# A linear-attention recurrence with a token and channel mixer: block triangular inverse, whole-partition evictions and a remade instruction order

## The chip, the cores and the metric

The kernel runs on one core of a Trainium2 chip. The metric is the device time of one execution in microseconds. The core's engines are TensorE (PE in the profile; PEld is its weight load), VectorE (DVE), ScalarE (ACT), GpSimd (POOL) and SyncE (SP), which issues most DMAs.

## The reference

Two parts follow one another. The first is a gated recurrence over 768 time steps for 4 batches and 8 heads with a 40 x 40 state. The second is a mixer over tokens and channels.

```python
def _attn_ref(r, k, v, w, a, b):           # each 4 x 8 x 768 x 40, float32
    state = zeros(B, H, D, D)
    for t in range(S):
        y[:, :, t] = einsum('bhd,bhde->bhe', r_t, state)
        Sa = einsum('bhde,bhe->bhd', state, a_t)
        state = state * w_t[:, :, None, :] - einsum('bhd,bhe->bhde', Sa, b_t)
        state = state + einsum('bhd,bhe->bhde', v_t, k_t)

def _moe_ref(x, w_tok1, w_tok2, w_ch1, w_ch2):   # x is y as 4 x 768 x 320
    h = relu(x.transpose(0, 2, 1) @ w_tok1) @ w_tok2       # 768 -> 256 -> 768
    u = x + h.transpose(0, 2, 1)
    h2 = relu(u @ w_ch1) @ w_ch2                            # 320 -> 1536 -> 320
    return u + h2
```

## The kernel before

**Chunks.** The 768 steps of a batch are cut into 12 chunks of 64, so there are 48 chunks in all, handled two by two as 24 pairs. Inside a chunk the recurrence is written with matrices: a 64 x 64 strictly triangular matrix per head must be inverted, and then a chunk needs a few matmuls and one state from the chunk before. Two heads stand on top of one another in the partitions: rows 0 to 39 hold one, rows 64 to 103 the other, and four such pairs of heads lie side by side.

**Preparation (t_pre, t_a).** For a pair, running products of the gates are formed by a scan (L552, L645), and the inputs are scaled by them (AB and KBp at L491, on DVE or POOL as the settings p_a and p_k say for each batch). Matmuls of L715 give the products px, whose two halves go to XT (masked, L727), NB (L733, L735) and Dg. Dg holds the diagonal 32 x 32 blocks. They stand alternately in the first and in the second 32 columns, and so four evictions of 32 partitions each bring them over (L746 on ACT or L748 on DVE).

**The solve (t_solve).** The chunks are solved in eight sets (of 4, 6, 6, 6, 6, 6, 6 and 8 chunks). DVE transposes the diagonal blocks (DT, L785) and inverts them: fifteen steps by rows, each a product (L808) and a sum (L810) over two 16 x 16 blocks at a time, of 2t^2 elements in step t. From the fourth set on, DVE also joins the 16 x 16 blocks to 32 x 32 (L823, L825, L836, L839); in the first three sets TensorE does that (merge). Two transposes give TBn and TBt (L871, L866).

**The chain (t_chain, t_s, t_rm, t_y).** For every chunk: z from XT, W, AB and the state (L1046), its eviction ZS (L1068, L1070), U and its transpose (L1082, L1085) in two PSUM banks, one for each of the two heads of a pair, U's two evictions to W (L1095, L1096), the transpose's two evictions to VT (L1166), and the new state ST (L1124, L1126, L1133). A copy of the state is spread into a block form (SS, L1152). VT and RB give RM (L1183), which is masked (L1200, or copied by ACT and masked by POOL at L1210 as rmp says), and L1237 and L1242 give y.

**The mixers (t_mlp).** One for each batch, started when its twelve chunks are done; the last one takes its tokens as they come. TensorE works with float32r operands split into a high and a low part. Settings say where an eviction goes: hdp (of a hidden tile's low part: DVE at L1640, or ACT and POOL at L1635) and c2p (of the second product: DVE at L1680, or ACT at L1674 and POOL at L1677), each with one number for each batch. The split weights are made in the kernel too (t_piece): 32 pieces are loaded by SP (L1321), converted by ACT, DVE (L1334, L1335, L1337) and POOL (L491), and stored to DRAM by SP (L1349).

**The order.** The program's order on every engine is made by a planner in the kernel's own Python. It simulates the engines with fixed prices, gives every step a rank (mostly in units of chunks) and lets each engine take the ready step of the lowest rank. The settings K hold ranks, spans, buffer counts and the choice of engines. A step that lists both ACT and DVE goes to the one that can take it. The conversion of weights has a gate:

```python
yield K_ready[min(K["conv_after"], NPR - 1)]
```

Of the kernel before, what the change touches and what calls it, by code (L numbers as in the profile page):

```python
# [24 lines left out]
LAT = {"PE": 190.0, "ACT": 210.0, "DVE": 130.0, "POOL": 150.0, "SP": 40.0, "SWD": 100.0}  # L25


K = dict(kw=4300.0, kwn=2, kw1=188.93925028732068, wug=10.0, ld0=0.6317250924768794, ldw0=2.1173303662595164,
         fgap=293.89554076183873, keep=3800.0, entry=3700.0, cold=0, hold=2428.165163486685, la=2.175877794961337,
         lw=-0.14323384525040384, le=1051.2152564940388, la_pe=-1.466665252232031, lw_pe=-37.533348810551956,  # L30
         lat=[200.0, 150.0, 145.0, 90.0], aff=1.4651042617773267, sets=[4, 6, 6, 6, 6, 6, 6, 8], nxt=8, nkp=2, nkb=12,
         rmp=[0, 0, 2, 0], hdp=[0, 1, 1, 1], c2p=[0, 0, 0, 1], npt=4, ld=6.038928624718252, ldv=4.00699059428611,
         pl=[-0.9477378132052551], ptl=3.6069776451328477, xtl=1.8544356360912841, kbl=-1.3723067761040764,
         op1=('ACT','DVE',), slack=-13908.358498323609, evm=15.481077541396273, slack_c=3496.0790885208608, p_a=[1, 2,
         1, 0], p_k=[0, 1, 1, 0], solve=[3.4390776166284533, 1.7006518949949656, 4.274466296951854, 2.435219810738553,
         3.4275080414655226, 5.510007117082695, -4.084092431783224, 0.1424821572249326], solve_span=9.61372691238832,
         atomic=1, a=8.22737306035122, a_span=3.1925291387789234, b=0.280588932000626, chain=-0.267542847460926,
         pu=-0.4315673334223724, rml=-1.6506651065553348, nw2=3, nvt=3, nrb=3, nrm=3, nss=2, evac=-4.311312911607387,
         y=-1.9244399780387127, utr=-6.460258455178398, pem=3, mrg=2.9201745296420394, ea=10, w=3, c=2, m=2, fill=300,
         alt_c=0, fill_cols=2692.2446469651372, mlp=[12.176995908837672, 28.35767213986017, 33.82155643447318,  # L40
# [1827 lines left out]
```

## Time and profile before

| | |
|---|---|
| time, median of 3 runs | 823.57 us (818.12 to 823.77) |
| the profiled execution's own time | 824.24 us |
| its span | 822.5 us |
| TensorE busy (matmuls) | 706.1 us, 86%, 14474 matmuls |
| TensorE weight loads | 633.0 us, 77% |
| DVE busy | 616.4 us, 75%, 1372 instructions |
| ACT busy | 338.9 us, 41%, 976 |
| POOL busy | 230.6 us, 28%, 252 |
| DMA | 129.22 MB, mean 157 GB/s |

The span runs from the first to the last instruction. Matmuls are pipelined, so a busy TensorE isn't one at its peak. Busy shares are means over the whole; the stages differ.

### The profile page before, as it was taken

How to read it: one execution, taken by the hardware profiler on the slowest of the kernel's cores; microseconds unless marked ns; L12 is line 12 of the kernel's file. 1: busy time of each engine (PE TensorE's matmuls, PEld its weight loads, DVE VectorE, ACT ScalarE, POOL GpSimd, SP SyncE). 2: the span in 40 equal slices, each digit the busy share in tenths (PEclk: the TensorE clock that was granted, in tenths of full speed). 3: DMA queues.
4: the chain of work that ended last, by engine and by line, in shares of the span. 5: the costliest groups of instructions: out<-in, count | busy, mean ns of one | idle time of the engine just before them, and what ended most of it. 6: DMA issues, size and time to landing. Idle time of an engine off the chain costs nothing.

```text
span 822.5 us, 33224 instructions
## 1 busy us (share of the span) xinstructions
PE 706.1 (86%) x14474; PEld 633.0 (77%) x14474; DVE 616.4 (75%) x1372; ACT 338.9 (41%) x976; POOL 230.6 (28%) x252
## 2 busy tenths in 40 slices
PE   3178757779887998999988899999999999999996
PEld 2167647668776887888877779888888888889996
DVE  6898898886778995998898789984499855445222
ACT  4237444434457334344344564544443222333221
POOL 4017655555655211012122022212101110102231
PEclk9999999999999997999997999999999999999999
DMA  9345773566679542445384464453664323445341
GB/s 248 90 145 146 225 225 110 174 190 182 199 232 299 170 160 85 153 128 162 109 269 134 138 187 146 140 172 96 195 197 128 116 79 106 140 136 164 113 147 52
DMA packets 61416, 129.22 MB, mean 157 GB/s; under 512 B 6864, under 2 KB 40912, under 8 KB 58192
## 3 DMA queue, kind: packets, MB, share of 16 engines
q1 hardware_dynamic: 54928, 79.85, 32.9%
q0 software_dynamic: 6336, 47.19, 17.6%
q8 instruction: 115, 1.88, 1.0%
q14 instruction: 37, 0.30, 0.1%
HBM read 108.33 MB, written 18.68 MB: 154 GB/s over the span
## 4 chain that ended last, share of the span: by engine, by line
PE 45%; DVE 29%; DMA 11%; issue 8%; ACT 3%; POOL 2%; SPq 1%; DVEq 0%; POOLq 0%; ACTq 0%
PE bkm L1505 8%; PE bkm L1616 7%; PE bkc L1505 4%; PE bkw L1616 4%; DMA cv_c<-in_moe_w_ch_dram 3%; PE bkw L367 3%; PE bkw L715 3%; DVE tmp L808 2%; DMA sG<-cv_c 2%; DVE Tl L810 2%; PE bkc L1082 2%; PE bkw L1183 2%; DMA sT<-cv_t 2%; PE bkc L1111 2%; DVE tmp_y L836 2%
## 5 line engine op out<-in xcount | busy, mean ns | idle before, releaser
L1616 PE MATMUL bkm<-ut,wg_c 128*128 128x384 f32 x560 | 120.3, 352 | 4.0 <-DVE hd L1640 1.4
L1505 PE MATMUL bkm<-wg_c,hd 128*128 128x320 f32 x621 | 110.3, 322 | 4.0 <-DVE hd L1640 2.6
L1616 PEld LDWEIGHTS bkm<-ut,wg_c 128*128 128x128 f32 x560 | 95.5, 189 | 9.0 <-DVE hd L1640 2.2
L1505 PEld LDWEIGHTS bkm<-wg_c,hd 128*128 128x128 f32 x621 | 92.7, 190 | 9.2 <-DVE hd L1640 4.8
L491 POOL TENSOR_TENSOR cv_c<-cv_c 128x384 f32<-128x384 f32 (+3 forms) x72 | 70.7, 998 | 53.7 <-ACT cv_c L1339 21.3
L1625 ACT ACTIVATE hd<-bkm 128x384 fp32r<-128x384 f32 x70 | 34.4, 491 | 115.8 <-PE bkm L1616 107.3
L1183 PE MATMUL bkw<-RB,VT 40*64 40x64 f32 x1536 | 51.9, 258 | 7.0 <-ACT VT L1166 4.6
L1439 POOL DMA_DIRECT2D wg_c<-sG x32 | 18.2, 569 | 138.3 <-PE bkm L1505 53.6
L1082 PE MATMUL bkc<-ZS,TBD 64*64 64x40 f32 x768 | 44.7, 257 | 11.9 <-DVE ZS L1070 6.0
L1680 DVE TENSOR_TENSOR x<-bkm,x 128x320 f32<-128x320 f32 x69 | 33.4, 485 | 26.6 <-PE bkm L1505 26.1
L1082 PEld LDWEIGHTS bkc<-ZS,TBD 64*64 64x64 f32 x768 | 37.0, 165 | 20.9 <-DVE ZS L1070 7.7
L1635 POOL TENSOR_TENSOR hd<-h,hd 128x384 fp32r<-128x384 f32 x24 | 25.2, 1049 | 89.5 <-issue 57.7
L367 PE MATMUL bkw<-ident,KBp 104*128 104x104 f32 x192 | 32.4, 329 | 20.7 <-issue 7.3
L1183 PEld LDWEIGHTS bkw<-RB,VT 40*64 40x64 f32 x1536 | 41.0, 163 | 10.9 <-ACT VT L1166 5.1
L808 DVE TENSOR_TENSOR tmp<-Tl,DT 128x2 f32<-128x2 f32 (+14 forms) x120 | 46.0, 383 | 2.2
L1242 PE MATMUL yb<-KT,RM 128*64 128x40 f32 x768 | 45.2, 244 | 0.7 <-POOL RM L1210 0.5
L491 POOL TENSOR_TENSOR AB<-AB,w 104x512 f32<-104x512 f32 x15 | 20.0, 1331 | 87.6 <-DVE w L552 85.3
L367 PEld LDWEIGHTS bkw<-ident,KBp 104*128 104x128 f32 x192 | 25.9, 186 | 23.8 <-issue 13.3
L1242 PEld LDWEIGHTS yb<-KT,RM 128*64 128x64 f32 x768 | 41.3, 163 | 1.1 <-POOL RM L1210 0.8
L810 DVE TENSOR_REDUCE Tl<-tmp 128x2 f32<-128x2 f32 (+14 forms) x120 | 38.6, 322 | 2.4
L1085 PE MATMUL bkc<-TBD,ZS 64*40 64x64 f32 x768 | 39.5, 254 | 0.7 <-issue 0.7
L715 PE MATMUL bkw<-AB,KBp 40*64 40x64 f32 x1408 | 37.2, 272 | 3.0 <-DVE XT L727 1.6
(184 smaller groups left out, 1783.8 us busy)
## 6 DMA issues: line engine op xcount, KB each, us to landing
wg_c<-sG POOLq DMA_DIRECT2D x16, 1152.0 KB, 6.4
wg_c<-sG POOLq DMA_DIRECT2D x16, 960.0 KB, 5.3
KBp<-in_kbT_dram SPq DMA_DIRECT2D x24, 448.0 KB, 4.7
wg_t<-sT POOLq DMA_DIRECT2D x8, 1152.0 KB, 6.1
W<-in_vt_dram SPq DMA_DIRECT2D x48, 160.0 KB, 3.2
w<-in_wT_dram SPq DMA_DIRECT2D x24, 224.0 KB, 2.9
wr<-in_wT_dram SPq DMA_DIRECT2D x24, 224.0 KB, 2.8
AB<-in_aT_dram SPq DMA_DIRECT2D x24, 224.0 KB, 3.7
```

The source lines that it names most:

```text
L367: nc.tensor.matmul(out_, lhsT=in_, rhs=idn, start=True, stop=True, is_transpose=True)
L491: return [(e, Port(60 + f * n / 0.96 if e == "DVE" else 140 + 2.24 * n), lambda e=e: engines[e].tensor_tensor(out=out_(), in0=a_(), in1=b_ ...
L715: nc.tensor.matmul(d["px"][i][0][o0:o0 + 64, z, p, :], lhsT=KBp[q][rows(r), p, z, i ^ r, :], rhs=AB[q][rows(r), p, z], start=True, stop=True)
L808: lambda tmp: tt(out=vw(tmp), in0=tv[:, :, 0:t, 0:t], in1=dv[:, :, t, 0:t].unsqueeze(2).to_broadcast([128, 2, t, t]), op=ALU.mult),
L810: lambda tmp: nc.vector.tensor_reduce(out=tv[:, :, 0:t, t], in_=vw(tmp), axis=AX.X, op=ALU.add),
L1082: nc.tensor.matmul(ub[r][0][bs, 0, p, 0:D], lhsT=oq["tbd"][bs, z, p, :], rhs=d["zs"][bs, p, :], start=True, stop=True)
L1085: nc.tensor.matmul(ub[r][0][rows(r), 1, p, :], lhsT=d["zs"][bs, p, :], rhs=oq["tbd"][bs, z, p, :], start=True, stop=True)
L1183: nc.tensor.matmul(bk[r][0][i * 64:i * 64 + 64, p, :], lhsT=o["vt"][rows(r), int(i != r), p * C:p * C + C], rhs=o["rb"][rows(r), p * C:p * ...
L1242: nc.tensor.matmul(py[g - 1][z * 64:z * 64 + 64, h, :], lhsT=RMs[g - 1 + z][:, h, :], rhs=st[g - 1 + z]["kb"][:, h, :], start=zero, stop=z ...
L1505: nc.tensor.matmul(d[key], lhsT=lhs(i, a_), rhs=rhs(i, b_), start=i == 0 and j == 0, stop=i == n - 1 and j == 2)
L1616: nc.tensor.matmul(pt, lhsT=mm_[q][0], rhs=mm_[q][1], start=q == 0, stop=q == len(mm_) - 1)
L1625: nc.scalar.activation(out=hid[key][:, 0], in_=pt, func=AF.Relu)
```

## The change

- **The inverse.** Row steps run only to 8 columns, on four 8 x 8 blocks at once (4t^2 elements in step t, t from 1 to 7). Then a copy of 128 elements and four steps of 512 elements (two "left", two "right", each a product and a sum) give the off-diagonal 8 x 8 blocks of the 16 x 16 ones.
- **Diagonal blocks.** One eviction of all 128 partitions brings the first 32 columns, multiplied by a factor for each partition that is -1 or 0; the other blocks are added from NB, multiplied by a factor that is 1 or 0 (e4).
- **State spread.** Both evictions read all 104 partitions and multiply by a 0/1 factor for each partition.
- **U transposed.** One PSUM bank holds U of both heads, the other holds the transposes; one eviction of all partitions goes to VT, and each bank is given back on its own.
- **Matmul rows.** The operands of several matmuls now take rows 0 to 63 and 64 to 103 or 111, where it was 40 rows of each; the rows between are zero in one of the operands.
- **The order.** Prices in the planner (DMA latencies, some instructions, TensorE's forms) and nearly all ranks are others. Settings by batch: c2p, hdp, rmp, p_k; conv_after is 1 and was 3. A form of the XT eviction that goes over ACT and POOL exists (xtp), and isn't used.

The long lists of numbers are shortened and rounded here.

```diff
-LAT = {... "SP": 40.0, "SWD": 100.0}
+LAT = {... "SP": 500.0, "SWD": 400.0}
...
-K = dict(kw=4300.0, ... keep=3800.0, entry=3700.0, ... nkb=12, rmp=[0, 0, 2, 0], hdp=[0, 1, 1, 1], c2p=[0, 0, 0, 1],
-         p_k=[0, 1, 1, 0], ... ea=10, fill_cols=2692, mlp=[12.18, 28.36, 33.82, 56.89], mlp_span=[13.5, 8.5, 12.4, 84.4],
-         conv_t=9.89, conv_t_span=-57.57, conv_c=4.67, conv_c_span=14.81, conv_after=3)
+K = dict(kw=3600.0, ... keep=3600.0, entry=3450.0, ... nkb=11, rmp=[0, 0, 2, 1], xtp=[0, 0, 0, 0], hdp=[1, 1, 1, 1], c2p=[0, 3, 3, 1],
+         p_k=[0, 0, 2, 0], ... ea=8, fill_cols=4332, mlp=[10.76, 28.78, 33.44, 51.80], mlp_span=[17.6, 7.9, 14.1, 89.7],
+         conv_t=9.96, conv_t_span=-56.49, conv_c=4.13, conv_c_span=17.91, conv_after=1)
...
+    def wrows(r, n=LP):
+        return slice(r * 64, 64 if r == 0 else n)
...
-                        nc.tensor.matmul(d["px"][i][0][o0:o0 + 64, z, p, :], lhsT=KBp[q][rows(r), p, z, i ^ r, :],
-                                         rhs=AB[q][rows(r), p, z], start=True, stop=True)
+                        nc.tensor.matmul(d["px"][i][0][o0:o0 + 64, z, p, :], lhsT=KBp[q][wrows(r), p, z, i ^ r, :],
+                                         rhs=AB[q][wrows(r), p, z], start=True, stop=True)
...
-        def e3(b, e):
-                sl, c0 = slice(b * L, b * L + L), (b & 1) * L
-                dst, src = Dgs[si % 2][sl, ci * NP:(ci + 2) * NP], kb_[sl, :, c0:c0 + L]
+        def e3(e):
+            dst, src = Dgs[si % 2][:, ci * NP:(ci + 2) * NP], kb_[:, :, 0:L]
+            if e == "ACT":
+                return ("ACT", act(256), lambda: nc.scalar.activation(out=dst, in_=src, func=AF.Copy, scale=mev[:, 0:1]), tb)
...
+        def e4():
+            dst = Dgs[si % 2][:, ci * NP:(ci + 2) * NP]
+            return ("DVE", Port(dve(256)), lambda: nc.vector.scalar_tensor_tensor(out=dst, in0=o["nb"], scalar=mod[:, 0:1], in1=dst, op0=ALU.mult, op1=ALU.add))
...
-        now = yield [[e3(b, "ACT"), e3(b, "DVE")] for b in range(4)] + [("DVE", dve(256), e2, tb) if ea else ("ACT", act(256), e2, tb)]
+        now = yield [[e3("ACT"), e3("DVE")], ("DVE", dve(256), e2, tb) if ea else ("ACT", act(256), e2, tb)]
         P.rel(tb, now)
+        now = yield [e4()]
...
-                    return tmp[:, 0:2 * t * t].rearrange("p (q j s) -> p q j s", q=2, j=t)
+                    return tmp[:, 0:4 * t * t].rearrange("p (q j s) -> p q j s", q=4, j=t)
...
+            def left8(q):
+                return step(
+                    lambda tmp: tt(out=cube(tmp), in0=dv[:, q, 8:16, 0:8].unsqueeze(2).to_broadcast(sh8),
+                                   in1=tv[:, q, 0:8, 0:8].unsqueeze(1).to_broadcast(sh8), op=ALU.mult),
+                    lambda tmp: nc.vector.tensor_reduce(out=d["Y"][:, 2 + q].rearrange("p j t -> p t j"), in_=cube(tmp), axis=AX.X, op=ALU.add),
+                    512, f"tmp{i}_l{q}", 1.1)
...
-            steps = [row(t) for t in range(1, 16)]
+            steps = [row(t) for t in range(1, 8)] + [[("DVE", Port(210), t22)]]
+            steps += [left8(0), left8(1), right8(0), right8(1)]
...
-            ub = yield from banks("c", [128, 2, NP, C], [f"u{g}", f"ut{g}"])
+            (u_, uk), (t_, tk) = yield from banks("c", [128, NP, C], [f"u{g}", f"ut{g}"])
...
-                (nc.scalar.copy if e == "ACT" else nc.vector.tensor_copy)(out=SS[g + 1][rows(r), :, r], in_=p_[rows(r)])
+                    nc.scalar.activation(out=SS[g + 1][:, :, r], in_=p_[0:DP], func=AF.Copy, scale=mhd[:, r:r + 1])
...
-        now = yield [[uc(r, "ACT"), uc(r, "DVE")] for r in range(2)]
-        yield u_ev
-        for _, k_ in ub:
-            P.rel(k_, now)
+        now = yield [[uc("ACT"), uc("DVE")]]
+        P.rel(tk, now)
```

## Rows read from the trace of the kernel before

**Rows 1.** Stretches: length, busy us (instructions) of each engine, PEclk, DMA share, GB/s

```profile
0.00:267.00 267.00, 184.11 (x5132) 165.02 (x5132) 219.88 (x488) 125.90 (x350) 132.73 (x141) 1.00 0.64 189
267.00:823.00 556.00, 521.97 (x9346) 467.97 (x9344) 396.56 (x885) 213.03 (x627) 97.85 (x112) 0.97 0.46 141
735.00:823.00 88.00, 80.75 (x548) 78.81 (x545) 26.72 (x59) 25.38 (x67) 19.82 (x25) 0.98 0.38 122
20.00:61.00 41.00, 18.82 (x500) 16.48 (x498) 37.10 (x79) 11.74 (x36) 4.44 (x4) 1.00 0.40 119
```

**Rows 2.** Waits of TensorE, 0 to 267 us: total us, times, longest us

```profile
PE bkw L919 <- DVE TBn L871: 22.6, 2, 17.5
```

**Rows 3.** Waits of TensorE, 267 to 823 us

```profile
PE bkc L1082 <- DVE ZS L1070: 4.1, 5, 1.9
```

**Rows 4.** L715, min/median/max ns in three stretches, and one stretch

```profile
L715 PE MATMUL bkw<-AB,KBp x448: 283/311/366, 63.0 to 248.3; 40*64 40x64 f32 x150
L715 PE MATMUL bkw<-AB,KBp x64: 311/311/344, 319.9 to 321.6; 40*64 40x64 f32 x64
L715 PE MATMUL bkw<-AB,KBp x320: 218/218/268, 466.2 to 560.6; 40*64 40x64 f32 x160
317.20:327.50 10.30, 10.30 (x220) 9.10 (x219) 4.94 (x10) 4.49 (x13) 0.00 (x0) 0.50 0.21 64
```

**Rows 5.** Timeline of DVE in the first solve: start us, length us

```profile
28.02 0.11 DVE L808 TENSOR_TENSOR tmp<-Tl,DT 128x2 f32<-128x2 f32 x1
...
32.59 0.37 DVE L808 TENSOR_TENSOR tmp<-Tl,DT 128x200 f32<-128x200 f32 x1
...
33.38 0.41 DVE L808 TENSOR_TENSOR tmp<-Tl,DT 128x242 f32<-128x242 f32 x1
...
37.54 0.63 DVE L808 TENSOR_TENSOR tmp<-Tl,DT 128x450 f32<-128x450 f32 x1
...
38.74 0.16 DVE L643 TENSOR_TENSOR D<-rq,PC 104x8 f32<-104x8 f32 x1
```

**Rows 6.** Groups by line and shape: busy us, mean ns, idle before

```profile
L746 ACT ACTIVATE Dg<-bkw 32x256 f32<-32x256 f32 x76 | 28.5, 375 | 18.6 <-PE bkw L715 17.9
L989 ACT COPY ET<-bkw 128x256 f32<-128x256 f32 x24 | 8.8, 367 | 7.1 <-PE bkw L983 6.7
L965 ACT ACTIVATE TBD<-TBt,blk 128x256 f32<-128x256 f32 x18 | 8.8, 506 | 9.4 <-DVE TBt L866 3.5 <-DVE TBt L939 3.1 <-DVE rq L640 1.9
L1335 DVE SCALAR_TENSOR_TENSOR cv_t<-cv_t 128x384 int32<-128x384 int32 x8 | 4.6, 573 | 0.6 <-ACT cv_t L1333 0.6
L1166 ACT COPY VT<-bkc 40x256 f32<-40x256 f32 x59 | 21.6, 366 | 1.0 <-DVE W L1096 0.2
L1166 DVE COPY VT<-bkc 40x256 f32<-40x256 f32 x37 | 15.6, 422 | 2.3 <-ACT W L1095 1.2
L1680 DVE TENSOR_TENSOR x<-bkm,x 128x320 f32<-128x320 f32 x69 | 33.4, 485 | 26.6 <-PE bkm L1505 26.1
L1677 POOL TENSOR_TENSOR x<-x,c 128x320 f32<-128x320 f32 x8 | 7.0, 871 | 32.1 <-ACT c L1674 32.1
L1635 POOL TENSOR_TENSOR hd<-h,hd 128x384 fp32r<-128x384 f32 x24 | 25.2, 1049 | 89.5 <-issue 57.7 <-ACT h L1632 31.8
L491 POOL TENSOR_TENSOR KBp<-KBp,wr 104x1024 f32<-104x1024 f32 x12 | 29.8, 2486 | 30.2 <-DVE wr L645 20.1 <-DMA KBp<-in_kbT_dram 5.0 <-PE bkc L1046 3.7
```

**Rows 7.** Groups by line: two operations of one size, over the whole span

```profile
L1126 DVE TENSOR_TENSOR ST<-bkc,ST 104x160 f32<-104x160 f32 x40 | 12.6, 316 | 9.8 <-PE bkc L1111 8.1 <-issue 1.3 <-ACT sp L1465 0.2
L1133 DVE TENSOR_TENSOR ST<-ST,PC 104x160 f32<-104x160 f32 x40 | 19.4, 486 | 0.6
```

**Rows 8.** Timeline around the gate of the conversion and the first state

```profile
16.93 1.23 DVE L491 TENSOR_TENSOR KBp<-KBp,wr 104x1024 f32<-104x1024 f32 x1 [1.56 <-DMA KBp<-in_kbT_dram]
...
54.05 2.91 SPq L1321 DMA_DIRECT2D cv_t<-in_moe_w_tok_dram  x4
...
73.61 0.33 DVE L1124 TENSOR_TENSOR ST<-bkc,PC 104x160 f32<-104x160 f32 x1 [0.88 <-PE bkc L1111]
```

More of the change, by code (lines that the diff above doesn't have):

```diff
@@ L24 @@
         "Q": (262.0, 340.0)}
[L25 to L40, printed above, removed]
-         56.88923782707786], mlp_span=[13.530525442548209, 8.457019380212113, 12.416974889480139, 84.37794635100765],
-         conv_t=9.890090295257227, conv_t_span=-57.567106844583016, conv_c=4.670000090481311,
-         conv_c_span=14.8116671529059, conv_after=3)
@@ L333, in run @@
             left[0] -= 1
-            left[1] = max(left[1], (end or t0 + ns) + (LATP[self.form][not self.warm] if e == "PE" else self.lat[eng]))
+            left[1] = max(left[1], (end or t0 + ns) + (LATP[self.form][not self.warm] if e == "PE" else self.lat[eng] + 1600.0 * (eng == "SP" and t[0].gi_code.co_name == "t_piece")))
             if left[0] == 0:
@@ L423, in tile_kernel @@
         nc.gpsimd.memset(blk0[q * 64:q * 64 + L], 1.0)
+    mev, mod = ctile([128, 1], "mev"), ctile([128, 1], "mod")
+    nc.gpsimd.tensor_scalar(out=mev, in0=blk0, scalar1=-1.0, scalar2=None, op0=ALU.mult)
+    nc.gpsimd.tensor_scalar(out=mod, in0=blk0, scalar1=-1.0, scalar2=1.0, op0=ALU.mult, op1=ALU.add)
+    mhd = ctile([DP, 2], "mhd")
+    nc.gpsimd.memset(mhd, 0.0)
+    for h in range(2):
+        nc.gpsimd.memset(mhd[h * 64:h * 64 + D, h:h + 1], 1.0)
     PC = ctile([DP, NG, NP], "PC")
@@ L573, in sq @@
                 nc.scalar.activation(out=jk, in_=d["wr"], func=AF.Square, accum_out=CE[bi][1][:, j:j + 1])
-            now = yield [("ACT", 525, sq)]
+            now = yield [("ACT", 616, sq)]
             P.set(sq_ev, now)
@@ L1143, in f @@
                 for r in range(2):
-                    nc.tensor.matmul(p_[rows(r), p, :], lhsT=ST[g + 1][rows(r), p, :], rhs=sel[rows(r), :], start=True, stop=True)
+                    nc.tensor.matmul(p_[rows(r), p, :], lhsT=ST[g + 1][wrows(r, DP), p, :], rhs=sel[wrows(r, DP), :], start=True, stop=True)
             return f
-        now = yield mm4([pu(p) for p in range(NP)], 77, 133, 94, "Q", 8)
+        now = yield mm4([pu(p) for p in range(NP)], 77, 133, 130, "Q", 8)
         P.set(PU_done[g + 1], now)
@@ L1182, in f @@
                     for i in range(2):
-                        nc.tensor.matmul(bk[r][0][i * 64:i * 64 + 64, p, :], lhsT=o["vt"][rows(r), int(i != r), p * C:p * C + C],
-                                         rhs=o["rb"][rows(r), p * C:p * C + C], start=True, stop=True)
+                        nc.tensor.matmul(bk[r][0][i * 64:i * 64 + 64, p, :], lhsT=o["vt"][wrows(r), int(i != r), p * C:p * C + C],
+                                         rhs=o["rb"][wrows(r), p * C:p * C + C], start=True, stop=True)
             return f
-        now = yield mm4([rr(p) for p in range(NP)], 142, 214, 258, "Q", 16)
+        now = yield mm4([rr(p) for p in range(NP)], 142, 214, 275, "Q", 16)
         P.rel(R_vt, now)
```

124 lines of the change are left out of this document (83 added, 41 removed).

## The prediction

> **What bounds the kernel now.** I read the stretches first: each row gives the length of the stretch, the busy time of TensorE, of its weight loads, of VectorE (DVE), ScalarE (ACT) and GpSimd (POOL), the granted clock and the DMA share [rows 1]. They show two different kernels. Up to 267 us TensorE is busy for 184.1 us and idle for 83, while DVE is busy for 219.9 us (82%), ACT for 125.9 and POOL for 132.7. From 267 us to the end TensorE is busy for 522.0 of 556 us and idle for 34. Of those 34, 7 lie in the stretch from 735 us, in which only the last mixer is left; the recurrence can move about 27.
>
> Next I read who keeps TensorE waiting. In the first stage one wait stands out: 22.6 us, in two pieces, the longer 17.5 us, for TBn, at the end of the triangular solve [rows 2]. In the second stage the longest entry is 4.1 us in five pieces [rows 3]. So a cheaper eviction can't win much by itself there, and in the first stage it wins only if it brings a solve or a chunk forward.
>
> Last I read TensorE's clock. The matmuls of L715 took 311 ns in the first stage. They took 311 ns also in a stretch where the granted clock was 0.50, and 218 ns in the stretch from 460 to 600 us [rows 4], in a stage whose mean is 0.97 [rows 1]. The 1.00 in the row of the first stage [rows 1] contradicts this; I go by the durations and take the first 267 us to run at the lower level. So work that moves out of that stage, or a stage that ends earlier, is worth its time, and a stretch at the lower level in the second stage costs 1 - 218/311 = 30% of its length.
>
> **The solve by rows to 8 and by blocks to 16.** The old rows run from 28.02 to 38.74 us in the first set: 10.7 us for fifteen steps, 2 x (1 + 4 + ... + 225) = 2480 elements in each of the two operations [rows 5]. The step of 200 elements takes from 32.59 to 33.38, 0.79 us; that of 450 from 37.54 to 38.74, 1.20 us. That is 0.00164 us an element and 0.46 us a step, and 15 x 0.46 + 2480 x 0.00164 = 11.0, close to 10.7. New: seven steps on four blocks, 4 x 140 = 560 elements, 7 x 0.46 + 0.92 = 4.1 us; four steps of 512, 4 x (0.46 + 0.84) = 5.2 us; one copy of 128 elements, which I put at 0.3. Sum 9.6, so 1.1 us a set is saved, 9 us of DVE over eight sets. In set 0 TensorE stands still for it, so 1.1 us counts in full. Sets 1 and 2 also lie in the first stage and the second piece of the TBn wait is one of theirs: 2 us of 2.2 counts. The five later sets are hidden behind a busy TensorE: 0, and at most 5.5 if that cover went.
>
> **Diagonal blocks in whole partitions.** Each of 24 pairs had four evictions of 32 partitions, 80 on ACT (76 of them in the row) at 375 ns and 16 on DVE, which I put at 0.4 us [rows 6]: 30 + 6.5 us. New are one eviction of 128 partitions and one addition from SBUF (e4). A longer partition range costs nothing on ACT: 256 elements on 32 partitions take 375 ns and on 128 partitions 367 (L989); with the factor read from a tile, as the new one has it, 506 (L965). So the eviction costs 9 to 12 us in all. The addition isn't in the trace; the nearest row is L1335, the same operation with 384 elements, 573 ns. Bounds for 256 elements are 0.28 and 0.57 us; I take 0.40, 9.6 us on DVE. ACT falls by about 19 us and DVE rises by about 3; at the lower bound it rises by nothing. A pair's path from matmul to solve shortens from five evictions in a row to three operations, some 0.7 us, which matters in set 0 alone and is inside the order's term below.
>
> **U transposed.** 96 copies become 48: 59 on ACT at 366 ns and 37 on DVE at 422 [rows 6], 37.2 us, halved: ACT -11, DVE -8. All of it in the second stage is covered. The two halves of U now share one PSUM bank, so their evictions go one behind the other; the bank is free without waiting for the low-ranked copy of the transpose. The one is worth up to +0.3 us a chunk, the other as much the other way; I take 0, with +/-4 us for the twelve chunks of the first stage. **State spread**: the same 88 evictions with a factor read from a tile; by L965 against L746 up to +0.13 us each, 11 us of ACT at most and hidden, since ACT is busy for less than half of either stage [rows 1]. **Whole row ranges in the matmuls** (64 or 48 rows for 40): the same count of instructions; L715 itself fixes no price for rows, so 0, bounds +/-3 us.
>
> **What the new settings move.** c2p for mixers 1 and 2 takes 48 additions from DVE (485 ns, L1680) to ACT and POOL (871 ns, L1677): DVE -23, POOL +42 [rows 6]. hdp for mixer 0: 8 subtractions to POOL at 1049 ns (L1635), +8, DVE -4. rmp for batch 3: 12 masks go from DVE to a copy on ACT and a product on POOL, of 256 elements and so below L1635's time: at most 1 us each, POOL +10, DVE some -5. p_k goes the other way: the six KBp products of batch 1 leave POOL (2.49 us each [rows 6]) for DVE (1.23 [rows 8]), +7 on DVE, half of it in the first stage; those of batch 2 may go to either. In the first stage alone DVE gets: rows -3.3, transposes -2.3, diagonal +1, KBp +3.7, so about -1. **The operations alone free nothing there**; the second stage loses some 30 us of DVE work, which TensorE's 27 us of idle time hardly sees.
>
> The moved POOL work can come back as waits. L1133 and L1126 are the same size; L1126 reads one input from PSUM and takes 316 ns in the mean; L1133 reads both from SBUF and takes 486, 170 ns more [rows 7]. The Trainium skill has a rule on this (SBUF — State Buffer, section Who interferes with whom): a DVE instruction with two SBUF inputs is locked out while a GpSimd instruction reads SBUF, one with a single SBUF input is not. The trace agrees, and the rule speaks against this change. Its price from rows is the second rival below.
>
> **The order.** Every instruction's place changes, and the trace of before shows no part of that; here I choose between bounds. In the first stage the conversion of weights waits until KBp of the fourth pair is done: its first four loads go out at 54.05 us. With conv_after 1 they may start when the second pair's is done, at 16.93 + 1.23 = 18.2 us [rows 8], at a time when POOL (4.4 of 41 us) and ACT (11.7) are mostly idle [rows 1]; the conversions of the channel weights are ranked later (last rank 21.5 for 19.0). SP is ahead of nothing it wasn't ahead of, but its queue then has cv_t loads beside those of w, AB and KBp. The product that makes the first state starts at 73.61 us [rows 8]. I take -5 us for the first stage, with bounds of -15 (a fifth of its idle time) and +12 (third rival below). In the second stage, -5 of the 27 us idle (bounds 0 and -12), and -3 for one stretch of 10.3 us at the lower clock [rows 4] that a denser order avoids (bounds -7 and +6, two stretches fewer or more).
>
> **Sum.** 824.24 - 1.1 - 2 - 5 - 5 - 3 = 808.1 us against the profiled execution, which lies 0.7 us above the median of the runs; forecast 808.
>
> **Rivals.** (1) Hidden: the removed work was covered, and the new order is as good as the old. Then only the solve's 3 us remain: 821. For it: TensorE is 94% busy from 267 us. Against it: 83 us of idle time before. (2) The port: some 60 us of POOL work is added in the second stage, 11% of it, to a POOL that was busy for 28% of the whole, so L1133's loss of 170 ns would grow by four tenths, 0.07 us. DVE has 885 instructions there [rows 1]; if half of them read two inputs from SBUF they lose 31 us together, which eats the relief, and if TensorE waits for a quarter of it the time is 824 - 3 + 8 = 829, within 1%. (3) **Slower: the conversions start too early.** DVE is busy for 37.1 of the 41 us from 20 to 61 us [rows 1]. Eight cv_t conversions need three DVE operations each, about 0.5 us apiece (L1335: 573 ns [rows 6]), 12 us in all. If the order puts them ahead of the preparation for the first two sets, the first state's product comes at 86 us and not 74, and everything behind it moves: 824 - 3 + 12 = 833. It decides as soon as more than some 8 of those 12 us stand before the first state. (4) The new solve does not get shorter, if strided 8 x 8 operands cost DVE more an element than rows do: nothing gained, 824.
>
> **How the numbers follow.** A measurement of this kernel tells 1% from no change. The forecast's case (better order, 790 to 815) gets 0.56; hidden 0.20 and the port 0.05 and no shorter solve 0.03 are within 1% (815.3 to 831.8), save 0.03 of them that reach below; the early conversions and other places where the order loses, 0.16, end at 832 and above. So faster 0.59, same 0.25, slower 0.16. The low end adds the order's better bounds, 824 - 3 - 15 - 10 - 5 = 791, taken as 790. The high end takes in rival 3 at 833.
>
> **What would show it.** In the trace after: L808 to L810 and the new block steps of set 0 together near 9.6 us; L746 with 24 evictions and e4 near 0.40 us; 48 copies to VT; the first stage's end (where L715's durations fall to 218 ns) some 8 us earlier than 267; TensorE idle in the second stage near 29 us. The first state's product later than 74 us would show rival 3; L1133's mean well above 486 ns would show rival 2. The prediction is wrong if the first stage doesn't shorten, or if the second gets more stretches at the lower clock.

## The result, and the profile after

The changed kernel takes 808.88 us (median of 4 runs, 807.97 to 811.02); the kernel before took 821.45 us beside it (4 runs, 818.12 to 823.77). The ratio is 0.987, with a 95% interval of 0.984 to 0.990: 1.3% faster. The forecast was 808.

First the stretches of the kernel after (length, busy us and instructions of TensorE, its weight loads, DVE, ACT and POOL, granted clock, DMA share, GB/s).

```profile
0.00:267.00 267.00, 190.64 (x5416) 168.65 (x5416) 225.21 (x488) 112.97 (x324) 107.75 (x127) 0.62 0.62 184
267.00:810.00 543.00, 504.12 (x9094) 452.57 (x9092) 357.24 (x755) 221.81 (x639) 172.21 (x189) 0.98 0.47 147
...
226.60:809.30 582.70, 536.12 (x9682) 481.67 (x9682) 393.69 (x837) 238.12 (x692) 183.36 (x201) 0.96 0.48 151
...
0.00:226.60 226.60, 158.63 (x4826) 139.54 (x4826) 188.76 (x406) 96.66 (x272) 96.59 (x115) 0.62 0.62 182
```

Against [rows 1] the first 267 us look almost alike: DVE is busy for 225 us where it was 220. A cut at a fixed time compares different work, though. A better cut is the moment at which mixer 0 starts, when ACT makes the first high part of its input: 250.5 us before, 226.6 us after. The same two stretches of the kernel before:

```profile
0.00:250.50 250.50, 173.03 (x4892) 154.66 (x4892) 203.97 (x438) 113.64 (x310) 124.39 (x133) 1.00 0.62 182
...
250.50:822.50 572.00, 533.05 (x9582) 478.33 (x9582) 412.47 (x935) 225.29 (x668) 106.19 (x119) 0.98 0.47 146
```

So the stage ahead of mixer 0 became **23.9 us shorter**: TensorE's busy time fell by 14.4 us with 66 matmuls (1.3%) fewer, its idle time by 9.5 (77.5 to 68.0). The stage behind it became **10.7 us longer**: 3.1 us busy, 7.6 us idle (39.0 to 46.6). The sum is the 13.2 us between the spans, 822.5 and 809.3.

The start of mixer 0 is itself a place in the order, and the new settings rank it earlier (mlp 10.76 for 12.18). A cut at the progress of the recurrence takes this out. The product U of the fifteenth chunk starts at 251.6 us before and at 235.9 after, that of the last chunk at 726.8 and at 707.7. The stretches ahead of the one and behind the other, before and then after:

```profile
0.00:251.60 251.60, 173.99 (x4921) 155.62 (x4922) 205.07 (x440) 114.68 (x313) 124.88 (x134) 1.00 0.62 183
726.80:822.50 95.70, 87.90 (x671) 84.93 (x671) 31.22 (x72) 26.57 (x71) 19.82 (x25) 0.98 0.40 128
```

```profile
0.00:235.90 235.90, 165.40 (x4962) 145.82 (x4962) 197.92 (x426) 100.72 (x285) 102.14 (x120) 0.62 0.63 185
707.70:809.30 101.60, 94.21 (x715) 90.84 (x709) 29.55 (x66) 29.77 (x79) 26.48 (x33) 0.98 0.40 126
```

After fourteen chunks the recurrence is **15.7 us ahead** (TensorE busy for 8.6 us less, idle for 7.1 less). At its last chunk it is 19.1 us ahead, so it gave nothing back. The part behind the last chunk is 5.9 us longer, with 44 matmuls more in it. Of the 23.9 us at mixer 0's start, 8.2 only stand for mixer 0's earlier place.

The waits of TensorE after, up to 267 us and behind it (total us, times, longest us):

```profile
PE bkw L368 <- DVE KBp L499: 13.7, 3, 7.0
PE bkw L970 <- DVE TBn L922: 8.5, 1, 8.5
...
PE bkc L1097 <- DVE ST L1177: 7.0, 7, 2.1
...
PE bkw L1034 <- issue: 3.5, 1, 3.5
PE bkm L1557 <- DVE hd L1692: 3.2, 5, 1.2
```

The wait for TBn, 22.6 us in two pieces [rows 2], is 8.5 us in one piece. The long piece stands at the first set's solve, before and after (TensorE's timeline: start, length, the wait ahead of it):

```profile
42.10 1.08 PE L919 MATMUL bkw<-TBn,Dg 32*32 32x32 f32 x64 [17.47 <-DVE TBn L871]
```

```profile
29.96 1.62 PE L368 MATMUL bkw<-ident,KBp 104*128 104x104 f32 x8 [6.97 <-DVE KBp L499]
...
41.98 1.07 PE L970 MATMUL bkw<-TBn,Dg 32*32 32x32 f32 x64 [8.48 <-DVE TBn L922]
```

It ends at nearly the same time in both; TensorE only does the next pair's products in the middle of it now. The short piece, 5.1 us, stood at the second set's solve and is gone, and that solve is what came forward. The transposes of DVE that frame it, after and then before (start, length):

```profile
65.39 2.00 DVE L810 STREAM_TRANSPOSE DT<-Dg 128x1024 f32<-128x1024 f32 x1
...
92.39 2.00 DVE L917 STREAM_TRANSPOSE TBt<-Tl 128x1024 f32<-128x1024 f32 x1
```

```profile
68.66 1.97 DVE L785 STREAM_TRANSPOSE DT<-Dg 128x1024 f32<-128x1024 f32 x1
...
119.24 1.91 DVE L866 STREAM_TRANSPOSE TBt<-Tl 128x1024 f32<-128x1024 f32 x1
```

From the first to the last it took 50.6 us before and takes 27.0 after. The solve itself is only about 1.5 us shorter (below); the rest is other work that DVE did in between. Up to the end of the last transpose, the conversions of the weights (busy us of DVE, ACT and POOL) stood there with these times, before (tile cv_c, then cv_t) and after (cv_t):

```profile
68.66:121.15 52.49, 6.37 (x8) 4.60 (x9) 6.81 (x6) 1.00 0.70 202
68.66:121.15 52.49, 8.16 (x15) 7.15 (x14) 21.60 (x20) 1.00 0.70 202
```

```profile
65.39:94.39 29.00, 5.37 (x14) 6.97 (x14) 16.07 (x16) 0.74 0.74 219
```

After, no cv_c is among them. So conversions on DVE fell from 14.5 us to 5.4, 9.2 of the 23.5 us by which this stretch is shorter, and DVE's idle time fell from 6.3 to 0.5.

What work left the first stage is seen in the rows of the tile cv_c, the conversion of the channel weights (busy us and instructions of DVE, ACT and POOL): ahead of mixer 0 before, ahead of it after, and behind it after.

```profile
0.00:250.50 250.50, 39.44 (x69) 33.12 (x69) 66.17 (x67) 1.00 0.62 182
```

```profile
0.00:226.60 226.60, 20.88 (x50) 24.09 (x50) 50.59 (x48) 0.62 0.62 182
...
226.60:809.30 582.70, 9.22 (x22) 10.43 (x22) 26.49 (x24) 0.96 0.48 151
```

Of 72 DVE instructions 69 stood ahead of mixer 0, now 50 do; that is 18.6 us of DVE less, more than the whole fall of 15.2 us (KBp from POOL brought 7.2 back). POOL has 15.6 us less of them there.

The price of the clock in the first stage stands in the durations of L726 (L715 before; min/median/max ns), ahead of mixer 0, and in the longest stretch there at the upper level (2.4 GHz):

```profile
L726 PE MATMUL bkw<-AB,KBp x576: 311/311/367, 31.5 to 200.1; 64*64 64x64 f32 x96, 48*64 48x64 f32 x96
L726 PE MATMUL bkm<-AB,KBp x128: 218/300/367, 16.8 to 21.9; 64*64 64x64 f32 x64, 48*64 48x64 f32 x64
...
68.84:82.49 13.65, 9.83 (x356) 8.07 (x352) 13.41 (x39) 5.30 (x17) 8.48 (x8) 1.00 0.75 215
```

Before, no such matmul was below 283 ns up to 248 us [rows 4]; after, 60 of the second pair's 64 take 218. The records after, which begin at 21.0 us, show the upper level for 34 us ahead of mixer 0, in six stretches, in which TensorE is busy for 23.0 us. With 311 ns for 218 these would be 32.8 us. By this estimate the clock makes 9.8 of the 14.4 us; what raised it is not shown. The 1.00 of the row before is no reading of that stretch: its first clock record is at 272.8 us.

Groups that answer to [rows 6] and [rows 7] (busy us, mean ns, idle before):

```profile
L1204 ACT ACTIVATE SS<-bkw,mhd 104x160 f32<-104x160 f32 x60 | 20.3, 392 | 8.1 <-PE bkw L1195 7.3 <-DVE ZS L1121 0.5
L755 ACT ACTIVATE Dg<-bkw,mev 128x256 f32<-128x256 f32 x21 | 9.9, 474 | 20.2 <-PE bkw L726 20.1
L746 ACT ACTIVATE NB<-bkw 128x256 f32<-128x256 f32 x20 | 7.5, 376 | 1.7 <-DVE Dg L756 1.7
L1220 ACT COPY VT<-bkc 112x256 f32<-112x256 f32 x10 | 3.7, 369 | 0.4 <-PE bkc L1137 0.4
L1184 DVE TENSOR_TENSOR ST<-ST,PC 104x160 f32<-104x160 f32 x40 | 21.2, 529 | 0.5
L1220 DVE COPY VT<-bkc 112x256 f32<-112x256 f32 x38 | 15.8, 416 | 14.2 <-PE bkc L1134 9.1 <-PE bkc L1137 4.9 <-ACT KT L692 0.3
L1177 DVE TENSOR_TENSOR ST<-bkc,ST 104x160 f32<-104x160 f32 x40 | 12.7, 318 | 10.7 <-ACT c L1726 6.1 <-ACT hd L1677 3.8 <-PE bkc L1162 0.6
L760 DVE SCALAR_TENSOR_TENSOR Dg<-NB,mod,Dg 128x256 f32<-128x256 f32 x24 | 12.7, 529 | 0.9 <-ACT NB L746 0.2
```

Whole partitions cost the copies to VT nothing a piece (416 ns for 422, 369 for 366), so there are 48 pieces for 96 at the same price each. The two evictions with a factor read from a tile cost more.

### The profile page after: what moved, and what is told of

The parts are those of the page before. It is cut to its first block, busy times and chain, and to the rows that moved or that the text cites. A ratio compares the mean times of both kernels' runs of the same rounds, so it can differ in the third digit from the quotient of the medians.

```text
span 809.3 us, 33171 instructions
## 1 busy us (share of the span) xinstructions
PE 694.8 (86%) x14508; PEld 621.2 (77%) x14508; DVE 582.5 (72%) x1242; ACT 334.8 (41%) x963; POOL 280.0 (35%) x316
## 4 chain that ended last, share of the span: by engine, by line
PE 52%; DVE 29%; DMA 7%; issue 7%; ACT 2%; POOL 1%; SPq 0%; DVEq 0%; ACTq 0%; POOLq 0%
PE bkm L1557 11%; PE bkm L1668 8%; PE bkw L1668 5%; PE bkc L1557 5%; PE bkw L368 2%; PE bkw L726 2%; PE bkc L1134 2%; PE bkc L1097 2%; DVE KBp L499 2%; PE bkw L1234 2%; PE yb L1293 2%; DMA w<-in_wT_dram 2%; DVE tmp_y L886 2%; DVE w L560 2%; DVE wr L653 1%
## 5 line engine op out<-in xcount | busy, mean ns | idle before, releaser
L1668 PE MATMUL bkm<-ut,wg_c 128*128 128x384 f32 x544 | 114.7, 349 | 0.9 <-DVE hd L1692 0.4
L1557 PE MATMUL bkm<-wg_c,hd 128*128 128x320 f32 x594 | 110.2, 327 | 4.5 <-DVE hd L1692 3.2
L499 POOL TENSOR_TENSOR cv_c<-cv_c 128x384 f32<-128x384 f32 (+3 forms) x72 | 77.1, 1084 | 96.5 <-ACT cv_c L1390 39.7
L1557 PEld LDWEIGHTS bkm<-wg_c,hd 128*128 128x128 f32 x594 | 90.7, 193 | 9.2 <-DVE hd L1692 4.6
L1729 POOL TENSOR_TENSOR x<-x,c 128x320 f32<-128x320 f32 x56 | 51.1, 913 | 114.0 <-ACT c L1726 113.7
L1234 PE MATMUL bkw<-RB,VT 64*64 64x64 f32 (+1 forms) x1536 | 47.5, 245 | 9.6 <-issue 5.1
L1687 POOL TENSOR_TENSOR hd<-h,hd 128x384 fp32r<-128x384 f32 x32 | 35.3, 1104 | 56.3 <-ACT h L1684 56.1
L368 PE MATMUL bkw<-ident,KBp 104*128 104x104 f32 x192 | 33.8, 322 | 22.6 <-DVE KBp L499 14.7
L1261 POOL TENSOR_TENSOR RM<-RM,upp 128x256 f32<-128x256 f32 x36 | 32.5, 915 | 57.8 <-ACT RM L1257 56.0
L1234 PEld LDWEIGHTS bkw<-RB,VT 64*64 64x64 f32 (+1 forms) x1536 | 36.9, 152 | 11.6 <-issue 5.4
L368 PEld LDWEIGHTS bkw<-ident,KBp 104*128 104x128 f32 x192 | 25.0, 178 | 27.0 <-issue 15.9
L1134 PE MATMUL bkc<-ZS,TBD 64*64 64x40 f32 x768 | 40.8, 251 | 4.6 <-ACT ZS L1119 2.9
L1668 PE MATMUL bkw<-ut,wg_c 128*128 128x384 f32 x224 | 43.0, 338 | 0.0
L499 POOL TENSOR_TENSOR AB<-AB,w 104x512 f32<-104x512 f32 x16 | 21.8, 1365 | 60.9 <-DVE w L560 47.7
L560 DVE TENSOR_TENSOR_SCAN w<-w,D 104x512 f32<-104x512 f32 x24 | 30.8, 1285 | 16.4 <-DMA w<-in_wT_dram 13.3
```

The costliest lines, as they stand in the source:

```text
L368: nc.tensor.matmul(out_, lhsT=in_, rhs=idn, start=True, stop=True, is_transpose=True)
L499: return [(e, Port(60 + f * n / 0.96 if e == "DVE" else 140 + 2.24 * n), lambda e=e: engines[e].tensor_tensor(out=out_(), in0=a_(), in1=b_ ...
L560: now = yield [("DVE", Port(1140), lambda: nc.vector.tensor_tensor_scan(out=d["P"], data0=d["P"], data1=D1, initial=0.0, op0=ALU.mult, op1 ...
L1134: nc.tensor.matmul(u_[bs, p, 0:D], lhsT=oq["tbd"][bs, z, p, :], rhs=d["zs"][bs, p, :], start=True, stop=True)
L1234: nc.tensor.matmul(bk[r][0][i * 64:i * 64 + 64, p, :], lhsT=o["vt"][wrows(r), int(i != r), p * C:p * C + C], rhs=o["rb"][wrows(r), p * C:p ...
L1557: nc.tensor.matmul(d[key], lhsT=lhs(i, a_), rhs=rhs(i, b_), start=i == 0 and j == 0, stop=i == n - 1 and j == 2)
```

## The experiments

Three views were tried first: that the earlier start of the token conversion (conv_after) makes the new order better; that the work moved to POOL or the evictions moved in the mixers do; and that neither settings nor instructions do by themselves, but the fit of one order to its instructions. Six kernels keep the after kernel's order to the instruction and put old instructions in their places; one does the reverse; five are planned anew by the same planner. "Planned anew" means that the planner laid out a new order for the edited settings, without any search for settings that suit it.

| run | order | instructions | median us | ratio to before, 95% interval | mixer 0 starts | from there to the end |
|---|---|---|---|---|---|---|
| before | old | old | 821.45 | 1 | 250.5 | 572.0 |
| after | new | new | 808.88 | 0.987 (0.984, 0.990) | 226.6 | 582.7 |
| e1_old_ops | new | old | 838.59 | 1.025 (1.020, 1.029) | 240.1 | 597.8 |
| e9_new_ops_old_order | old | new | 826.12 | 1.010 (1.006, 1.015) | 246.3 | 577.4 |
| e5_rows40 | new | new, 40 rows | 811.22 | 0.990 (0.986, 0.994) | 225.0 | 584.7 |
| e6_inv_old | new | new, old inverse | 816.54 | 0.998 (0.995, 1.001) | 231.4 | 583.5 |
| e7_diag_old | new | new, old diagonal | 806.31 | 0.986 (0.983, 0.990) | 228.0 | 578.6 |
| e8_u_old | new | new, old U, spread, rows | 824.86 | 1.010 (1.006, 1.013) | 227.6 | 597.6 |
| e10_diag_spread_old | new | new, old diagonal, spread | 811.06 | 0.991 (0.987, 0.994) | 224.5 | 583.1 |
| e2_conv_old | planned anew | new | 828.18 | 1.013 (1.007, 1.018) | 233.6 | 590.9 |
| e3_pk_old | planned anew | new | 828.19 | 1.010 (1.006, 1.014) | 232.3 | 596.2 |
| e4_evict_old | planned anew | new | 819.58 | 1.000 (0.997, 1.003) | 226.1 | 587.9 |
| e11_jitter | planned anew | new | 818.22 | 1.001 (0.998, 1.004) | 222.5 | 594.4 |
| e12_new_ops_old_settings | planned anew | new | 847.08 | 1.035 (1.030, 1.039) | 249.0 | 597.0 |

The last two columns are of the profiled execution, in us. The first four rows are four corners: old or new order with old or new instructions.

Most of the times fell outside the ranges that stand below. e3, e4, e5 and e11 landed in one. e1, e2, e9 and e12 came out above all of theirs, e8 above that of its theory 'instructions', e6 between two of its ranges, e7 just below its lowest, e10 between its two. So the theories are judged here by differences between runs and not by their ranges.

**Instructions and order.**

```diff
 # e1_old_ops: the after kernel's order, in each place the old instructions
-            return slice(r * 64, 64 if r == 0 else n)
+            return rows(r)
-            steps = [row(t) for t in range(1, 8)] + [[("DVE", Port(210), t22)]]
-            steps += [left8(0), left8(1), right8(0), right8(1)]
+            steps = [old(row(t), [t]) for t in range(1, 8)] + [[("DVE", Port(210), row16(8))]]
+            steps += [old(left8(0), [9, 10]), old(left8(1), [11, 12]), old(right8(0), [13, 14]), old(right8(1), [15])]
...
```

> The changed kernel with its order kept (the planner's steps and prices are untouched), but in each of the changed steps the old instructions are issued: inverse by fifteen rows, four evictions of a diagonal block, two copies for each transpose of U, state spread and matmuls by 40 rows. The bank layout of U stays new. Theory 'order' (the gain is the placing of work in the first stage, the instructions themselves freed some 3 us): 811 to 816 us, the first stage's second solve ends within 4 us of the changed kernel's 92 us. Theory 'work' (the gain is the removed instructions): 818 to 824 us, and that solve ends past 100 us.

```diff
 # e9_new_ops_old_order: the kernel before's order, in each place the new instructions
-            steps = [row(t) for t in range(1, 16)]
+            for t in range(1, 16):
+                pr = [("DVE", Port(60 + 2.2 * t * t), None), ("DVE", 62 + 2.08 * t * t, None)]
+                steps.append([(en, ns, new.pop(0) if new else (lambda: None)) for en, ns, _ in pr])
...
+        late.setdefault(si, []).append(e4)
```

> The kernel before with its own order kept (its planner's steps, prices and settings are untouched), but with the changed instructions in the old places: the inverse by rows to 8 and blocks to 16 in the first 23 of the 30 places, one eviction of the diagonal block in the first of four places with the additions from NB ahead of the set's transpose, one copy of U's transpose in the first of two places, the state spread and the matmul rows as changed. Theory 'instructions' (they are worth about 28 us in any order, as the four runs that put them back showed): 795 to 808 us. Theory 'fit' (they count only in an order planned for them; elsewhere the engines wait at their old places): 813 to 821 us.

With the new order alone (and the new bank layout of U) the kernel is 2.5% slower than before, with the new instructions alone 1.0% slower, with both 1.3% faster. The instructions are worth 1.025 - 0.987 = 3.8% in the order laid out for them and -1.0% in the old one; the two do not add up. In e9 the removed work is really gone (DVE is busy for 405 us behind 250 us, 413 before) and the first stage ends 4.2 us earlier, but what follows takes 5.4 us longer. The addition e4 stands there right ahead of the set's transpose, which is not where the new order has it. In these four corners the gain needs both. Whether an order searched for the old instructions would have won as much was not tested; the new order was laid out for the new ones.

**The parts, in the new order.**

```diff
 # e5_rows40
-            return slice(r * 64, 64 if r == 0 else n)
+            return rows(r)
 # e6_inv_old: the lines of `steps` as in e1_old_ops
 # e7_diag_old
-            dst, src = Dgs[si % 2][:, ci * NP:(ci + 2) * NP], kb_[:, :, 0:L]
+                for b in range(4):
+                    sl, c0 = slice(b * L, b * L + L), (b & 1) * L
+                    dst, src = Dgs[si % 2][sl, ci * NP:(ci + 2) * NP], kb_[sl, :, c0:c0 + L]
...
-            return ("DVE", Port(dve(256)), lambda: nc.vector.scalar_tensor_tensor(...))
+            return ("DVE", Port(dve(256)), lambda: None)
 # e8_u_old: rows(r) as in e5_rows40, the old copies of the state to SS, and
-                (...)(out=dst, in_=t_[0:LP])
+                for r in range(2):
+                    (...)(out=dst[rows(r)], in_=t_[rows(r)])
 # e10_diag_spread_old: the edits of e7_diag_old and the old copies of the state to SS
```

> The changed kernel with its order kept; only the matmuls' operands take 40 rows again instead of 64 and 40 or 48. Theory 'clock' (the wider rows keep TensorE's clock at the upper level; without them the long stretches at the lower level that the kernel with all old instructions showed come back): 815 to 825 us and over 45 us at the lower level after 250 us. Theory 'instructions' (the loss of that kernel came from its longer evictions and solves): 806 to 812 us and some 25 us at the lower level, as in the changed kernel.

> The changed kernel with its order kept; only the inverse goes by fifteen rows again, in the places of the new steps. Theory 'instructions': 1.1 us later at the first solve's end, 811 to 816 us in all. Theory 'clock': 807 to 811 us. If the solve alone carries most of the loss: 820 us or more.

> The changed kernel with its order kept; only the diagonal blocks are again brought over by four evictions of 32 partitions, in the place of the one, and the addition from NB is left out. Theory 'instructions': some 1.2 us more for each pair on ACT or DVE, in line before the solve; 813 to 820 us. Theory 'clock': 807 to 811 us.

> The changed kernel with its order kept; the transpose of U is copied in two halves again, the state spread and the matmul rows go by 40 rows. Theory 'instructions': 48 more copies of some 0.3 us, each in an engine's queue ahead of others; 812 to 820 us. Theory 'clock': as the run with 40 rows alone.

> The changed kernel with its order kept, with the diagonal blocks again by four evictions (no addition from NB) and the state spread again by two copies of 40 rows without a factor; the inverse, the transpose of U and the matmul rows stay changed. Theory 'instructions': a copy without the factor is 0.1 us shorter on ACT (287 against 392 ns), 88 times, and the addition on DVE is gone, so 799 to 805 us, faster than the changed kernel. If the spread is the part that cost 19 us in the run with the old U copies and spread: 815 us or more.

The rows are worth 0.3%, within the intervals. The diagonal blocks and the spread are worth nothing that these runs can tell: both put back (e10) give 0.991, the diagonal alone 0.986.

The old inverse costs 1.1% by the medians (0.5 to 1.7% by the intervals) and 5.6 us by the spans. The table says where: 4.8 us ahead of mixer 0, 0.8 behind. DVE's two transposes ahead of and behind set 0's solve in e6 stand 16.07 us apart (14.48 after, which has the same other work between them):

```profile
26.02 1.89 DVE L810 STREAM_TRANSPOSE DT<-Dg 128x1024 f32<-128x1024 f32 x1
42.09 1.85 DVE L932 STREAM_TRANSPOSE TBn<-Tl 128x1024 f32<-128x1024 f32 x1
```

The old U, with its two copies to VT, is the dear part: 2.3%. Here the table says the reverse: 1.0 us ahead of mixer 0, 14.9 us behind it. The rows cost 0.3% (e5), the spread at most some 0.5% (e10 against e7), so most of it is put down to the copies; no run put back the copies alone. The group of e8:

```profile
L1218 DVE COPY VT<-bkc 40x256 f32<-40x256 f32 x76 | 31.8, 418 | 12.0 <-PE bkc L1134 9.0 <-PE bkc L1137 1.8 <-ACT KT L692 0.3
```

DVE has 38 copies more, 16 us. The y of the same two chunks come at 309.5 and 501.1 us in the kernel after and at 312.0 and 515.6 us in e8. The stretch between them in e8 and after:

```profile
312.00:515.60 203.60, 181.51 (x3893) 158.68 (x3891) 181.68 (x375) 86.71 (x263) 61.09 (x63) 0.94 0.54 167
```

```profile
309.50:501.10 191.60, 173.50 (x3885) 152.08 (x3884) 172.99 (x364) 85.77 (x259) 64.64 (x63) 0.98 0.58 179
```

It takes 12.0 us longer for 11 instructions and 8.7 us more on DVE. DVE is busy for 89 to 90% of it in both, where the mean of the second stage that I had looked at is 71% [rows 1]. TensorE's waits for a state that DVE makes grow along with it, in e8 to this (whole span; 8.4 us, 9 times, after):

```profile
PE bkc L1097 <- DVE ST L1177: 14.5, 12, 3.8
```

TensorE's busy time grows by 8.0 us of the 12.0 for the same matmuls, at a granted clock of 0.94 for 0.98. Behind 250 us the lower level (1.2 GHz) was granted for 49.6 us in e8, 23.7 after, and 34.1 with the old rows alone (e5). How much of e8's loss is the clock's and how much the copies' own is not separated.

**The settings.**

```diff
 # e2_conv_old
+K.update(conv_t=9.890090295257227, conv_t_span=-57.567106844583016, conv_c=4.670000090481311, conv_c_span=14.8116671529059, conv_after=3)
 # e3_pk_old
+K.update(p_k=[0, 1, 1, 0])
 # e4_evict_old
+K.update(c2p=[0, 0, 0, 1], hdp=[0, 1, 1, 1], rmp=[0, 0, 2, 0])
 # e11_jitter: one rank of the chain, moved by 0.03
+K.update(chain=-0.03318755955648236)
 # e12_new_ops_old_settings: all settings of the kernel before, and its prices for DMA
-LAT = {... "SP": 500.0, "SWD": 400.0}
+LAT = {... "SP": 40.0, "SWD": 100.0}
+K.update(...)
```

> The changed kernel planned anew with the conversion's gate and ranks of before (conv_after 3 and the four conv ranks). Theory 'order, by the conversion' (the gain is that less conversion work lies between the second set's transposes): 817 to 824 us, that solve takes over 40 us and the last conversion stores come before 275 us. Theory 'work', or an order that gains elsewhere: 807 to 813 us.

> The changed kernel planned anew with p_k of before (KBp of batches 1 and 2 on POOL). Theory 'POOL' (KBp products of 2.5 us on POOL held back DVE and the conversion in the first stage): 815 us or more, and DVE's conversion operations in the first stage rise by some tenths of a microsecond each. Theories 'order, by the conversion' and 'work': 806 to 813 us.

> The changed kernel planned anew with c2p, hdp and rmp of before, so that the evictions of the second stage go back to DVE. Theory 'second stage' (relief of DVE behind TensorE is worth something): 814 us or more. Theories 'order' and 'work' in the first stage: 806 to 812 us, since TensorE was 94% busy there.

> The changed kernel planned anew with one rank (chain) moved by 0.03 of a chunk, which means nothing by itself. Theory 'search' (any plan anew that was not searched loses 10 us or more, so that the runs with single settings of before say nothing of those settings): 815 to 830 us. Theory 'settings' (those settings were worth the 11 to 19 us each): 806 to 812 us.

> The changed kernel's instructions, planned anew with all settings and DMA prices of before. Theory 'instructions': 803 to 812 us. Theory 'search': 818 to 835 us, as the runs with single settings. Theory 'settings of the second stage': 818 to 822 us, the changed kernel's first stage with the old second one.

The runs e2 to e4 lose 1.3 to 2.6% against the kernel after. e11 changes a rank by three hundredths of a chunk and loses 1.5%. So a fresh order can cost that much by itself, and none of the runs e2 to e4 shows that its setting was worth something. Only one such meaningless change was tried, so how far the cost of a fresh order varies is not known.

What these runs do show is how the first stage goes along with the conversions. DVE's conversions of the channel weights ahead of mixer 0, by the tile cv_c up to mixer 0's start, in e12 and in e2:

```profile
0.00:249.00 249.00, 40.03 (x69) 32.84 (x69) 69.11 (x69) 0.64 0.63 183
```

```profile
0.00:233.60 233.60, 21.83 (x48) 22.37 (x48) 47.15 (x47) 0.68 0.61 176
```

| run | cv_c on DVE ahead of mixer 0 | mixer 0 starts |
|---|---|---|
| before | 69, 39.4 us | 250.5 |
| e12_new_ops_old_settings | 69, 40.0 us | 249.0 |
| e9_new_ops_old_order | 69, 41.8 us | 246.3 |
| e1_old_ops | 50, 21.6 us | 240.1 |
| e2_conv_old | 48, 21.8 us | 233.6 |
| e3_pk_old | 54, 30.0 us | 232.3 |
| after | 50, 20.9 us | 226.6 |
| e4_evict_old | 50, 21.6 us | 226.1 |
| e11_jitter | 50, 21.7 us | 222.5 |

Every kernel that keeps 69 of them in front starts mixer 0 at 246 us or later, whatever its instructions; every one that leaves some 20 for later starts it at 222 to 240. And each of the latter takes 578 to 598 us from there on, where the kernel before took 572.0; but e12, with 69 in front, takes 597.0 as well, so the conversions behind mixer 0 are not the only price there. The same two groups differ at the second set's solve: from its first to the end of its last transpose it takes 49.5 to 52.5 us in the three with 69, with 10.0 to 14.5 us of conversions on DVE in it, and 28.6 to 36.0 us with 5.3 to 7.1 in all the others. This goes together in every run, but no run moved the conversions and nothing else. Putting conv_after and the four ranks of the conversion back (e2) leaves the count at 48, so these settings did not move it; p_k and the evictions by themselves did not either. Which of the others did (the ranks of the mixers, the DMA prices) was not tried.

## Why the prediction was right, and where it was not

The sign, the size and the range held. The sum behind the size did not hold term by term, and that it met the result so closely is luck. By the profiled executions 16.1 us were forecast and 13.2 came. Up to the fifteenth chunk 15.7 us came where the sum has 8.1 for the first stage; from there on 2.5 us were lost where it has a gain of 8. The two errors nearly cancel. The low end of the range was also added up with 10 and 5 us where the bounds named are 12 and 7; with these it is 787.

- **"I take -5 us for the first stage" and "about -1" for DVE in it.** This step failed, by the row on cv_c. DVE lost 15.2 us of work ahead of mixer 0, and the stage became 23.9 us shorter, 15.7 by the fifteenth chunk. The text had noted that the conversions of the channel weights are ranked later and put no price on it. The bound of -15 holds by the chunks, where the solve has a part of the 15.7, and not by mixer 0's start. conv_after, from which I argued, did not move them: with the old value the count stays at 48 (e2). The token conversion did start at the gate, at 18.57 us.
- **"-5 of the 27 us idle" and "-3 for one stretch at the lower clock".** The first failed: from 267 us to the end of the span TensorE is idle for 38.2 us (33.5 before, 29 forecast). The second came in sum: behind 267 us the lower level was granted for 27.5 us before and 16.8 after, 10.7 us less, at 30% some 3 us. It is in five stretches where it was four, so the forecast's own sign of being wrong, more stretches at the lower clock, is met by their number and not by their length. The recurrence gave back nothing of the first stage; the 5.9 us that were lost lie behind the last chunk, where TensorE has 44 matmuls more. The conversions are over by 390 us, so they are not there.
- **"The first stage's end ... some 8 us earlier".** It came 12.8 us earlier: the product of mixer 0 that runs there (L1505, L1557 after) falls from 468 to 309 ns at 272.8 us before and at 260.0 after, where the upper level then holds for over 30 us.
- **"U transposed ... I take 0; all of it in the second stage is covered."** Failed in the new order: up to 15.9 us by spans (e8, with the old rows and spread in it), 14.9 of them behind mixer 0's start. I had read DVE's load as a mean of 71% over 556 us. Before, it was 88% from 250 to 560 us (272.4 of 310) and lower only behind that. The forecast that the copies would leave DVE by 8 us failed too: 38 of the 48 went to DVE, 15.8 us for 15.6, and ACT got the whole relief. In the old order all the new instructions together won nothing (e9).
- **The inverse, -1.1 and -2, the later sets 0.** The place was right, the size a little low: 4.8 us ahead of mixer 0 for 3.1, and 0.8 behind it (e6). Set 0's TBn came no earlier for it, though: DVE starts on it at 40.06 us, 40.08 before, because the new order puts other work between the steps. DVE's timeline in set 0's solve, the answer to [rows 5]:

```profile
27.50 0.17 DVE L836 TENSOR_TENSOR tmp<-Tl,DT 128x4 f32<-128x4 f32 x1
...
28.64 1.21 DVE L499 TENSOR_TENSOR KBp<-KBp,wr 104x1024 f32<-104x1024 f32 x1
29.77 0.22 DVE L836 TENSOR_TENSOR tmp<-Tl,DT 128x64 f32<-128x64 f32 x1
...
31.83 0.48 DVE L692 COPY KT<-bkw 128x320 f32<-128x320 f32 x1
32.23 0.35 DVE L838 TENSOR_REDUCE Tl<-tmp 128x28 f32<-128x196 f32 x1
...
33.60 0.69 DVE L738 TENSOR_TENSOR XT<-bkw,upp 128x512 f32<-128x512 f32 x1
34.21 0.41 DVE L744 TENSOR_SCALAR NB<-bkw 128x256 f32<-128x256 f32 x1
34.54 0.68 DVE L853 TENSOR_REDUCE Y<-tmp_l 128x64 f32<-128x512 f32 x1
35.13 0.48 DVE L760 SCALAR_TENSOR_TENSOR Dg<-NB,mod,Dg 128x256 f32<-128x256 f32 x1
35.52 0.68 DVE L851 TENSOR_TENSOR tmp_l<-DT,Tl 128x512 f32<-128x512 f32 x1
...
36.97 0.69 DVE L858 TENSOR_TENSOR tmp_r<-Y 128x512 f32<-128x512 f32 x1
...
38.41 0.69 DVE L858 TENSOR_TENSOR tmp_r<-Y 128x512 f32<-128x512 f32 x1
...
39.74 0.16 DVE L648 TENSOR_SCALAR rq<-ce 104x8 f32<-104x8 f32 x1
```

From 27.50 to 39.74 are 12.2 us, of which other work takes 1.13 (KBp), 0.40 (KT), 0.94 (XT and NB) and 0.39 (the addition e4), each from its start to the next step's. The 9.4 us left answer to the forecast's 9.6, with a pair of 512 elements at 1.44 us (36.97 to 38.41) where I had 1.30, and the row steps quicker than the formula.
- **Diagonal blocks, spread, rows at 0.** Right (e5, e7, e10). The addition e4 takes 0.53 us in the mean where I took 0.40; it lies inside the bounds of 0.28 and 0.57, and leaving it out gained nothing.
- **The rivals.** The conversions did not delay the first state: its product came at 69.0 us, not later than the 73.6 of before [rows 8]. The port: L1184 (L1133 before) rose from 486 [rows 7] to 529 ns with POOL busy for 280 us where it was 231, 40 x 0.043 = 1.7 us, so the sign was right and the size small. The trace shows how: of the 40, 12 overlapped a POOL operation before and 19 after. Those took 881 and 763 ns in the mean, the others 316 and 317. The Trainium skill (SBUF — State Buffer, section Who interferes with whom) has DVE's second SBUF input wait for a GpSimd read; L1177, with one input in PSUM, stayed at 318 ns (316), and takes 319 with a POOL operation beside it and 317 without, which agrees. Hidden (821) fell too.
- **What the form of the sum assumed.** It added instructions and order. The four corners say that they do not add: by such a sum of the corners the result would be 1.025 x 1.010 = 1.035, and it is 0.987. That e12, the new instructions planned by the old settings, is 3.5% slower points the same way; some of that is the cost of a fresh order.

Why time taken from DVE in a fixed order brings nothing (e7, e9, e10) and time added costs (e6, e8) is argued only: where the order on an engine is fixed, a shorter instruction helps only if the next is already free to start, while a longer one delays all behind it. No run separated that from the clock, which is lower in e8's stretch too. Open is also which settings moved the conversions, and whether a search with the old instructions would have found an order as good.
